# Softmax row statistics crossed between partition quadrants by VectorE instead of a TensorE product, and a new order of ScalarE's exponentials and roundings

## The chip, the core and the metric

The kernel runs on one core of a Trainium2 chip. The metric is the device time of one execution in microseconds (us). Three runs of the kernel before gave 2883.12, 2887.05 and 2887.52 us, median 2887.05 us.

Names in what follows: PE is TensorE's matmul row and PEld its weight load, DVE is VectorE, ACT is ScalarE, POOL is GpSimd, SP is the engine that issues most loads. Each engine runs its own instructions strictly in the order in which the program gives them, and engines wait for each other by semaphores. SBUF and PSUM have 128 partitions; a quadrant is 32 of them. L523 means line 523 of the kernel before.

## The reference, cut to what matters

A transformer block with adaptive layer norm. The change lies in the attention, where a softmax is taken over 512 keys:

```
h = layernorm(x) * (1 + ca) + sa
q = (h @ wq) as 32 heads of 128
k, v = the last 512 of 2048 cached positions, 16 heads, each used by 2 heads of q
p = softmax(q k^T * 128**-0.5)          # 2048 queries x 512 keys, per head
x = x + ga * ((p v) @ wo)
h = layernorm(x) * (1 + cb) + sb
x = x + gb * (relu(h @ W_gate) * (h @ W_up)) @ W_down
```

All data are float32. The kernel splits each operand of a product into a rounded part and a rest (hi and lo) and adds three products (hi hi, lo hi, hi lo), so each logical product is three matmuls.

## The kernel before, in words

The attention is cut into 128 units: a head and a block of 512 queries (32 heads, 4 blocks). The second half of the time is the gated MLP, which the change does not touch. All engines' orders are written out by hand; only the semaphores between them are put in by the framework. A list of timed steps (`step(name, t, ...)`, run by `run(u, k)` up to time 10u+k) puts the rest of the work (weight cuts, layer norms, gates of `wo`, MLP preparation) between the fixed parts of a unit.

One unit u, in the order of the loop at L1613:

- `s_half(u, 0)` and `(u, 1)` (L487): the scores, transposed, keys on partitions and queries on the free axis, in two PSUM tiles of 128 x 2 x 512 (pool psS, two buffers). Behind each, DVE takes a maximum with a 32x32 transposing reduction (L500), after which partition p of quadrant a holds, for column b, the maximum over the keys of that quadrant of query 32b + (p mod 32).
- `max_pre(u)` (L504): a small maximum over the four key tiles (L508), and the result spread into four masked copies, one per quadrant (L509).
- `sum_pre(u-1)` (L512): the same transposing reduction (L515) over the partial sums of the exponentials of the unit before.
- `qproj(u+1)`: 14 matmuls (L423) that make the next unit's queries.
- `spread(u)` (L519): one float32 product with the constant `quad` (L523), 80 columns. It adds up partitions that are equal modulo 32, so each quadrant receives what the four held: 64 columns for the masked maxima and 16 for the sums. It is PE's only work of this kind, and it stands in PE's order behind the 14 matmuls of `qproj`.
- `max_bc(u)` (L536): DVE's maximum over the four columns groups (L538), the reciprocal of the sums of u-1 (`sum_inv`, L528), and a 32x32 transpose that broadcasts the maximum to 128 x 512 (L551). For the units 0 to 3 and 127 (`by_pe`) the maximum is split into hi and lo (L544, L545), transposed (L546), rounded by ACT (L549) and subtracted by PE (L564).
- a piece of the output projection `wo` (12 matmuls, L637), `pv_half(u-1, 0)` (L610 to L612).
- `exp_half(u, 0)` and `(u, 1)` (L559): DVE subtracts the maximum (L568), ACT takes the exponential (L570). `hi_half` (L555) is ACT's rounding (L557); that of half 0 stands in ACT's order between the two exponentials, that of half 1 behind both.
- `sum_bc(u-1)` (L530): the broadcasting transpose of the reciprocal (L533); `q_lo(u+1)` (L477): the rest of the next queries (L479), which the next scores need; `ksum_op` (L579): DVE adds two of the four key tiles (L583), then POOL the other two (L586).
- `pv_half(u-1, 1)`, a second piece of `wo`, `o_mul(u-1)` (L618), then `lo_half` (L575): POOL subtracts the rounded from the exact exponentials (L577), 128 x 1024 per half. The product with v of unit u, in the unit after, needs them (L612).

PSUM pool psM has two buffers, taken in turn by `qps` (next queries), `qm` (the tile of the spread) and `pv`.

Of the kernel before, what the change touches and what calls it, by code (L numbers as in the profile page):

```python
# [28 lines left out]
PE0, PE1, MLP0 = 4, 1, 8  # L29
# [4 lines left out]
def kernel(  # L34
# [13 lines left out]
    nc = tc.nc  # L48
# [3 lines left out]
    cp = ctx.enter_context(tc.tile_pool(name="cp", bufs=1))  # L52
# [6 lines left out]
    bp = ctx.enter_context(tc.tile_pool(name="bp", bufs=3))  # L59
    op = ctx.enter_context(tc.tile_pool(name="op", bufs=3))  # L60
    xp = ctx.enter_context(tc.tile_pool(name="xp", bufs=3))
    sp = ctx.enter_context(tc.tile_pool(name="sp", bufs=2))
# [13 lines left out]

    ones = cp.tile([P, P], F32, name="ones")
    nc.vector.memset(ones, 1.0)

    ints = bp.tile([P, P], I32, tag="bc", name="ints")  # L80
    quad = cp.tile([P, P], F32, name="quad")
    nc.gpsimd.iota(ints, pattern=[[1, P]], base=P, channel_multiplier=-1)
    nc.vector.tensor_scalar(ints, ints, 31, None, op0=ALU.bitwise_and)
    nc.vector.tensor_scalar(quad, ints, 0.0, None, op0=ALU.is_equal)
    inta = bp.tile([P, 4], I32, tag="bc", name="inta")
    mask = cp.tile([P, 4], F32, name="mask")
    nc.gpsimd.iota(inta, pattern=[[-32, 4]], base=0, channel_multiplier=1)
    nc.vector.tensor_scalar(inta, inta, 5, None, op0=ALU.arith_shift_right)
    nc.vector.tensor_scalar(mask, inta, 0.0, None, op0=ALU.is_equal)

    intc = bp.tile([P, P], I32, tag="bc", name="intc")
    minus = cp.tile([P, P], F32R, name="minus")
# [355 lines left out]
    NU = HKV * NQB * 2  # L448
# [30 lines left out]
        nc.vector.scalar_tensor_tensor(qlo[u], qst.pop(u)[0], SCALE, qhi[u].bitcast(F32),  # L479
                                       op0=ALU.mult, op1=ALU.subtract)  # L480

    st_, t4, t5, pt, hi_, lo_, bc, rb, rinv, ks_, pvps, done, o, bps = ({} for _ in range(14))

    def by_pe(u):
        return u < PE0 or u >= NU - PE1

    def s_half(u, h):  # L487
        g, qb, hd = unit(u)
        k = ks[g]
        t = psS.tile([P, 2, 512], F32, tag="s", name=f"s{u}_{h}")  # L490
        st_[u, h] = t
        for j in range(2):
            kt = 2 * h + j
            ps = t[:, j, :]
            nc.tensor.matmul(ps, k[:, kt, :], qhi[u], start=True, stop=False)  # L495
            nc.tensor.matmul(ps, k[:, 4 + kt, :], qhi[u], start=False, stop=False)  # L496
            nc.tensor.matmul(ps, k[:, kt, :], qlo[u], start=False, stop=True)  # L497
        if h == 0:
            t4[u] = sp.tile([P, 4, 16], F32, tag="t4", name=f"t4_{u}", bufs=1)
        nc.vector.tensor_reduce(t4[u][:, 2 * h:2 * h + 2, :].rearrange("p k b -> p (k b)"),  # L500
                                t.rearrange("p k (b j) -> p (k b) j", j=32),
                                axis=AX.X, op=ALU.max, apply_transpose=True)

    def max_pre(u):  # L504
        t5[u] = sp.tile([P, 5, 16], F32, tag="t5", name=f"t5_{u}", bufs=1)
        bps[u] = psM.tile([P, 512], F32, tag="mm", name=f"qm{u}")
        t = bps[u][:, 128:144]
        nc.vector.tensor_reduce(t, t4.pop(u).rearrange("p k b -> p b k"), axis=AX.X, op=ALU.max)  # L508
        nc.vector.tensor_tensor(t5[u][:, 0:4, :], mask[:, :, None].to_broadcast([P, 4, 16]),  # L509
                                t[:, None, :].to_broadcast([P, 4, 16]), op=ALU.mult)  # L510

    def sum_pre(u):  # L512
        if u + 1 == NU:
            t5[NU] = sp.tile([P, 5, 16], F32, tag="t5", name=f"t5_{NU}", bufs=1)
        nc.vector.tensor_reduce(t5[u + 1][:, 4, :],  # L515
                                ks_.pop(u).rearrange("p (b j) -> p b j", j=32),
                                axis=AX.X, op=ALU.add, apply_transpose=True)

    def spread(u):  # L519
        a, b = (0 if u < NU else 4), (5 if u else 4)  # L520
        if u == NU:
            bps[u] = psM.tile([P, 512], F32, tag="mm", name=f"qm{u}")
        nc.tensor.matmul(bps[u][:, a * 16:b * 16], quad,  # L523
                         t5.pop(u)[:, a:b, :].rearrange("p a b -> p (a b)"), start=True, stop=True)

    def sum_inv(u):
        r = rinv[u] = sp.tile([P, 16], F32, tag="ri", name=f"ri{u}", bufs=1)
        nc.vector.reciprocal(r, bps[u + 1][:, 64:80])  # L528

    def sum_bc(u):  # L530
        r = rinv.pop(u)
        rb[u] = bp.tile([P, 512], F32, tag="bc", name=f"rb{u}")
        nc.vector.transpose(rb[u].rearrange("p (b j) -> p b j", j=32),  # L533
                            r[:, :, None].to_broadcast([P, 16, 32]))

    def max_bc(u):  # L536
        r = bps[u][:, 256:272] if by_pe(u) else sp.tile([P, 16], F32, tag="r", name=f"r{u}", bufs=1)
        nc.vector.tensor_reduce(r, bps[u][:, :64].rearrange("p (a b) -> p b a", a=4), axis=AX.X, op=ALU.max)  # L538
        if u:
            sum_inv(u - 1)  # L540
        m = bp.tile([P, 512], F32, tag="bc", name=f"mb{u}")
        if by_pe(u):
            rr = sp.tile([P, 16, 2], F32R, tag="rr", name=f"rr{u}", bufs=1)
            nc.vector.tensor_copy(rr[:, :, 0], r)  # L544
            nc.vector.tensor_sub(rr[:, :, 1], r, rr[:, :, 0].bitcast(F32))  # L545
            nc.vector.transpose(m.rearrange("p (b s t) -> p b s t", s=2, t=16),  # L546
                                rr.bitcast(F32)[:, :, :, None].to_broadcast([P, 16, 2, 16]))
            bc[u] = bp.tile([P, 512], F32R, tag="bc", name=f"mr{u}")
            nc.scalar.copy(bc[u], m)  # L549
        else:  # L550
            nc.vector.transpose(m.rearrange("p (b j) -> p b j", j=32),  # L551
                                r[:, :, None].to_broadcast([P, 16, 32]))
            bc[u] = m

    def hi_half(u, h):  # L555
        hi_[u, h] = pp.tile([P, 2, 512], F32R, tag="hi", name=f"hi{u}_{h}")
        nc.scalar.copy(hi_[u, h], pt[u, h])  # L557

    def exp_half(u, h):  # L559
        t = st_.pop((u, h))  # L560
        p = pp.tile([P, 2, 512], F32, tag="p", name=f"p{u}_{h}")
        if by_pe(u):
            for j in range(2):
                nc.tensor.matmul(t[:, j, :], minus, bc[u], start=False, stop=True,  # L564
                                 skip_group_check=True)
            nc.scalar.activation(p, t, AF.Exp, bias=0.0, scale=1.0)
        else:
            nc.vector.tensor_tensor(p, t, bc[u][:, None, :].to_broadcast([P, 2, 512]),  # L568
                                    op=ALU.subtract)
            nc.scalar.activation(p, p, AF.Exp, bias=0.0, scale=1.0)  # L570
        pt[u, h] = p
        if h == 0:
            hi_half(u, 0)

    def lo_half(u, h):  # L575
# [949 lines left out]
    mlp = mlp_slots()  # L1525

    def last_unit():
        spread(NU)
        sum_inv(NU - 1)
        sum_bc(NU - 1)  # L1530
        o_mul(NU - 1)

# [64 lines left out]
    def run(u, k):  # L1597
        t = 10 * u + k
        while sched and sched[-1][0] <= t:
            fn, args = sched.pop()[2:]  # L1600
            fn(*args)
# [11 lines left out]
    for u in range(NU):  # L1613
        run(u, 0)
        if u > 1 and u % 2 == 0:
            o_hi(u - 2)
            o_lo(u - 2)
        s_half(u, 0)
        s_half(u, 1)
        run(u, .5)  # L1620
        max_pre(u)
        if u:
            sum_pre(u - 1)
        run(u, 1)
        if u + 1 < NU:
            qproj(u + 1, 0, 14)
        else:
            piece(at[10 * u + 1])
            pv_part(u - 1, False)
        run(u, 2)  # L1630
        spread(u)
        max_bc(u)
        if u + 1 < NU:
            q_hi(u + 1)
        run(u, 3)
        if 10 * u + 3 in at:
            piece(at[10 * u + 3])
        if u > 1 and u % 2:
            o_hi(u - 2)
            o_lo(u - 2)  # L1640
        run(u, 4)
        if u + 1 == NU:
            pv_part(u - 1, True)
        elif u:
            pv_half(u - 1, 0)
        flush(pend_act)
        exp_half(u, 0)
        flush()
        run(u, 5)
        exp_half(u, 1)  # L1650
        if u:
            sum_bc(u - 1)
        if u + 1 < NU:
            q_lo(u + 1)
        ksum_op(u, 0)
        ksum_op(u, 1)
        run(u, 6)
        if 0 < u < NU - 1:
            pv_half(u - 1, 1)
        if 10 * u + 6 in at:  # L1660
# [67 lines left out]
```

## Time and profile before

The profiled execution took 2884.48 us; its span from the first to the last instruction is 2882.7 us, the rest of 1.8 us lies around it. The attention ends at about 1632 us.

| what | before |
|---|---|
| median of 3 runs | 2887.05 us |
| profiled execution, its span | 2884.48 us, 2882.7 us |
| granted TensorE clock, mean | 0.997 |
| ACT busy | 1496.2 us (52%) |
| L500 transposing maximum on DVE | 256 x 1244 ns |
| L568 subtraction of the maximum on DVE | 246 x 1218 ns |
| L570 exponential on ACT | 246 x 1056 ns |
| L557 rounding on ACT | 256 x 1051 ns |
| L577 subtraction for lo on POOL | 256 x 2399 ns |

A row of groups reads: line, engine, operation, output<-inputs, shapes, count, then busy us and mean ns of one, then the engine's idle time just before these instructions and what ended it. A row of the waits reads: engine, tile and line that waited, what it waited for, us in total, times, longest. A row of the timeline reads: start us, length us, engine, line, operation, output<-inputs, shapes, count of merged instructions, and in brackets the idle time before with what ended it.

### The profile page before, as it was taken

What the parts mean: (1) busy time and instruction counts of PE and PEld (TensorE: products, weight loads), DVE (VectorE), ACT (ScalarE), POOL (GpSimd) and SP (SyncE); (2) the same over time, 40 slices, a digit from 0 to 9 for tenths busy, and PEclk for the clock granted to TensorE, in tenths of its full rate; (3) what the DMA queues carried; (4) which work ended last, traced back from release to release, by engine and by line L of the source; (5) the groups of instructions that cost most, each with busy time, mean ns of one, the idle gap of its engine ahead of it and who ended that gap; (6) DMA issues with size and microseconds to landing.
All of it is one profiled execution on the core that took longest, in us unless ns stands there. A gap on an engine that the chain in (4) does not pass through costs nothing.

```text
span 2882.7 us, 41271 instructions
## 1 busy us (share of the span) xinstructions
PE 2839.4 (98%) x15214; PEld 2476.9 (86%) x15214; DVE 2149.1 (75%) x2967; ACT 1496.2 (52%) x2105; POOL 2115.0 (73%) x1564
## 2 busy tenths in 40 slices
PE   6999999999999999999999999999999999999999
PEld 5788888888888888888888888888888888888888
DVE  7778788888878888777889756676677466666666
ACT  5666666666676666666656444444444222222221
POOL 5688888888888889776778666787787356656553
PEclk9999999999999999999999999999999999999999
DMA  4012222222223223322244456666667944444442
GB/s 161 23 46 70 72 101 83 71 90 99 97 83 100 92 64 135 103 71 87 66 131 145 149 216 218 233 243 232 228 228 256 354 160 156 154 154 155 160 153 106
DMA packets 164362, 399.59 MB, mean 139 GB/s; under 512 B 15040, under 2 KB 61888, under 8 KB 164160
## 3 DMA queue, kind: packets, MB, share of 16 engines
q1 hardware_dynamic: 132912, 284.84, 30.1%
q10 hardware_dynamic: 31248, 112.11, 9.9%
q8 instruction: 121, 1.98, 0.3%
q14 instruction: 81, 0.66, 0.1%
HBM read 271.16 MB, written 154.57 MB: 148 GB/s over the span
## 4 chain that ended last, share of the span: by engine, by line
PE 90%; POOL 3%; DVE 2%; ACT 2%; DMA 2%; issue 1%; SPq 0%; ACTq 0%; POOLq 0%; DVEq 0%
PE gu L981 26%; PE wo L637 13%; PE qps L423 13%; PE md L637 8%; PE st_P L1083 6%; PE s L497 4%; PE s L496 4%; PE s L495 4%; PE pv L612 4%; PE pv L611 4%; PE pv L610 4%; PE qm L523 1%; POOL lo L577 1%; ACT p L570 0%; DVE ws L788 0%
## 5 line engine op out<-in xcount | busy, mean ns | idle before, releaser
L577 POOL TENSOR_TENSOR lo<-p,hi 128x1024 fp32r<-128x1024 f32 x256 | 608.7, 2399 | 1.1 <-ACT hi L557 1.1
L586 POOL TENSOR_TENSOR ks<-ks,p 128x512 f32<-128x512 f32 x256 | 343.8, 1343 | 270.6 <-ACT p L570 212.6
L500 DVE TRANSPOSE_TENSOR_REDUCE t<-s 128x32 f32<-128x1024 f32 x256 | 316.6, 1244 | 136.9 <-PE s L497 125.6
L981 PE MATMUL gu<-hop_B,wop 128*128 128x512 f32 x1512 | 374.5, 391 | 0.2 <-DMA wop<-wk_P 0.2
L981 PEld LDWEIGHTS gu<-hop_B,wop 128*128 128x128 f32 x1512 | 275.0, 188 | 50.5 <-ACT lflh L966 0.9
L981 PE MATMUL gu<-hop_T,wop 128*128 128x512 f32 x1260 | 316.0, 391 | 0.0
L423 PE MATMUL qps<-hTa,wA 128*128 128x512 f32 x1288 | 311.4, 392 | 4.2 <-DVE hTa L371 2.1
L637 PE MATMUL wo<-woga,ohi 128*128 128x288 f32 x1472 | 306.5, 301 | 0.0
L568 DVE TENSOR_TENSOR p<-s,mb 128x1024 f32<-128x1024 f32 x246 | 290.2, 1218 | 4.1
L423 PEld LDWEIGHTS qps<-hTa,wA 128*128 128x128 f32 x1288 | 242.8, 189 | 57.4 <-DVE hTa L371 4.2
L557 ACT CAST hi<-p 128x1024 fp32r<-128x1024 f32 x256 | 269.1, 1051 | 7.1
L570 ACT ACTIVATE p<-p 128x1024 f32<-128x1024 f32 x246 | 259.8, 1056 | 7.6 <-DVE p L568 7.3
L637 PE MATMUL md<-wogb,hhi 128*128 128x288 f32 x1280 | 258.9, 295 | 3.6 <-DVE acc L648 2.6
L981 PEld LDWEIGHTS gu<-hop_T,wop 128*128 128x128 f32 x1260 | 227.8, 188 | 38.9
L475 ACT ACTIVATE qhi<-qps 128x512 fp32r<-128x512 f32 x128 | 76.5, 597 | 340.4 <-PE qps L423 340.4
L637 PEld LDWEIGHTS wo<-woga,ohi 128*128 128x128 f32 x1472 | 239.2, 189 | 7.3
L648 DVE TENSOR_TENSOR acc<-md,acc 128x576 f32<-128x576 f32 x160 | 120.7, 755 | 160.8 <-PE md L637 160.3
L637 PEld LDWEIGHTS md<-wogb,hhi 128*128 128x128 f32 x1280 | 212.2, 188 | 16.6 <-DVE acc L648 4.3
L637 PE MATMUL wo<-woga,olo 128*128 128x288 f32 x736 | 217.4, 295 | 0.3 <-POOL olo L626 0.2
L1092 DVE TENSOR_TENSOR acc<-st_P,acc 128x576 f32<-128x576 f32 x160 | 121.0, 757 | 128.0 <-PE st_P L1083 128.0
L637 PE MATMUL md<-wogb,hlo 128*128 128x288 f32 x640 | 188.6, 295 | 0.0
L646 ACT COPY acc<-wo 128x576 f32<-128x576 f32 x233 | 148.2, 636 | 66.8 <-PE wo L637 60.4
(274 smaller groups left out, 7107.2 us busy)
## 6 DMA issues: line engine op xcount, KB each, us to landing
wop<-wk_P SPq DMA_DIRECT2D x133, 640.0 KB
wk_P<-wop ACTq DMA_DIRECT2D x119, 640.0 KB
wr<-wlay SPq DMA_DIRECT2D x68, 384.0 KB
rogb<-wd SPq DMA_DIRECT2D x68, 288.0 KB
againq<-akq SPq DMA_DIRECT2D x18, 640.0 KB
rwA<-wq SPq DMA_DIRECT2D x32, 320.0 KB
wlay<-wg SPq DMA_DIRECT2D x36, 256.0 KB
roga<-wo SPq DMA_DIRECT2D x32, 288.0 KB
```

What stands on the lines that cost most here:

```text
L423: return [lambda i=i, a=a, b=b: nc.tensor.matmul(ps, a, b, start=(i == 0), stop=(i == n - 1)) for i, (a, b) in enumerate(ops)]
L500: nc.vector.tensor_reduce(t4[u][:, 2 * h:2 * h + 2, :].rearrange("p k b -> p (k b)"), t.rearrange("p k (b j) -> p (k b) j", j=32), axis=AX ...
L557: nc.scalar.copy(hi_[u, h], pt[u, h])
L568: nc.vector.tensor_tensor(p, t, bc[u][:, None, :].to_broadcast([P, 2, 512]), op=ALU.subtract)
L570: nc.scalar.activation(p, p, AF.Exp, bias=0.0, scale=1.0)
L577: nc.gpsimd.tensor_sub(lo_[u, h], pt[u, h], hi_[u, h].bitcast(F32))
L586: nc.gpsimd.tensor_tensor(ks_[u], ks_[u], p[:, j, :], op=ALU.add)
L637: nc.tensor.matmul(ps[:, half, :H2], a[:, sl], w[b][:, cs], start=(n == 0 and seed is None), stop=(n == 5), skip_group_check=seed is not None)
L646: nc.scalar.copy(av, ps[:, :, :H2])
L981: nc.tensor.matmul(ps, a, c, start=s not in heir(m) and i == 0 and s not in seeds_of(m), stop=i == len(ops) - 1, skip_group_check=True)
L1083: nc.tensor.matmul(ps[:, j, :H2], x[:, sl], w[:, y, :], start=n == 0 and not second, stop=n == 2, skip_group_check=True)
L1092: nc.vector.tensor_tensor(t, ps[:, :, :H2], t, op=ALU.add)
```

## The change

It has three parts.

1. The constants `quad` and `mask` go, with two iotas of POOL and four small operations of DVE at the start. `max_pre`, `spread` and `sum_inv` go: per unit L508, L509, the product L523 and L538. In their place `cross(u)` does the crossing on DVE with reductions: the four per-tile maxima (16 columns each) and the sums (16 columns) of quadrants 2 and 3 are moved beside those of 0 and 1 (one operation, 64 partitions, 80 elements), then those of quadrant 1 beside quadrant 0 (32 partitions, 160 elements); quadrant 0 takes the maximum of 256 elements to 16 and the sum of 64 to 16; the two results (32 elements) are moved to quadrant 1, and then from 0 and 1 to 2 and 3. A move is a maximum over an axis of length one. `t4` and `t5` become one SBUF tile of 128 x 21 x 16.
2. `cross(u)` and `max_bc(u)` stand in the program right behind `sum_pre(u-1)`, ahead of `qproj(u+1)` and of the timed steps of 10u+1 and 10u+2. The reciprocal moves into `sum_bc`, behind both subtractions L568, in place, and directly ahead of the transpose L533.
3. For the units 5 to 125, ACT's rounding of half 0 moves behind the exponential of half 1.

```diff
+        nc.vector.tensor_reduce(t5[u][:, 8 * h:8 * h + 8:4, :],
                                 t.rearrange("p k (b j) -> p (k b) j", j=32),
                                 axis=AX.X, op=ALU.max, apply_transpose=True)
...
-    def max_pre(u):
...
-    def spread(u):
...
-    def sum_inv(u):
...
+    def move(dst, src):
+        nc.vector.tensor_reduce(dst, src[..., None], axis=AX.X, op=ALU.max)
+
+    def cross(u):
+        t = t5.pop(u)
+        v = t[:, 0:20, :].rearrange("p (k a) b -> p k a b", a=4)[:, (0 if u < NU else 4):(5 if u else 4)]
+        move(v[0:64, :, 1, :], v[64:128, :, 0, :])
+        move(v[0:32, :, 2:4, :], v[32:64, :, 0:2, :])
+        r = rr_[u] = t[:, 15:21:5, :]
+        if u < NU:
+            nc.vector.tensor_reduce(r[0:32, 1, :], t[0:32, 0:16, :].rearrange("p n b -> p b n"), axis=AX.X, op=ALU.max)
+        if u:
+            nc.vector.tensor_reduce(r[0:32, 0, :], t[0:32, 16:20, :].rearrange("p n b -> p b n"), axis=AX.X, op=ALU.add)
+        w = slice(0 if u else 1, 2 if u < NU else 1)
+        move(r[32:64, w, :], r[0:32, w, :])
+        move(r[64:128, w, :], r[0:64, w, :])
 
     def sum_bc(u):
-        r = rinv.pop(u)
+        r = rr_.pop(u + 1)[:, 0, :]
+        nc.vector.reciprocal(r, r)
...
     def max_bc(u):
-        r = bps[u][:, 256:272] if by_pe(u) else sp.tile([P, 16], F32, tag="r", name=f"r{u}", bufs=1)
-        nc.vector.tensor_reduce(r, bps[u][:, :64].rearrange("p (a b) -> p b a", a=4), axis=AX.X, op=ALU.max)
-        if u:
-            sum_inv(u - 1)
+        r = rr_[u][:, 1, :]
...
+    def late_hi(u):
+        return PE0 < u < NU - 2
...
-        if h == 0:
+        if h == 0 and not late_hi(u):
             hi_half(u, 0)
...
-        max_pre(u)
         if u:
             sum_pre(u - 1)
+        cross(u)
+        max_bc(u)
         run(u, 1)
...
-        spread(u)
-        max_bc(u)
         if u + 1 < NU:
             q_hi(u + 1)
...
         exp_half(u, 1)
+        if late_hi(u):
+            hi_half(u, 0)
```

More of the change, by code (lines that the diff above doesn't have):

```diff
@@ L78 @@
     nc.vector.memset(ones, 1.0)
[L80 to L89, printed above, removed]
     intc = bp.tile([P, P], I32, tag="bc", name="intc")
@@ L480, in q_lo @@
                                        op0=ALU.mult, op1=ALU.subtract)
-    st_, t4, t5, pt, hi_, lo_, bc, rb, rinv, ks_, pvps, done, o, bps = ({} for _ in range(14))
+    st_, t5, pt, hi_, lo_, bc, rb, rr_, ks_, pvps, done, o = ({} for _ in range(12))
     def by_pe(u):
@@ L498, in s_half @@
         if h == 0:
-            t4[u] = sp.tile([P, 4, 16], F32, tag="t4", name=f"t4_{u}", bufs=1)
-        nc.vector.tensor_reduce(t4[u][:, 2 * h:2 * h + 2, :].rearrange("p k b -> p (k b)"),
+            t5[u] = sp.tile([P, 21, 16], F32, tag="t5", name=f"t5_{u}", bufs=1)
+        nc.vector.tensor_reduce(t5[u][:, 8 * h:8 * h + 8:4, :],
                                 t.rearrange("p k (b j) -> p (k b) j", j=32),
                                 axis=AX.X, op=ALU.max, apply_transpose=True)
-    def max_pre(u):
[L505 to L510, printed above, removed]
@@ L512, in sum_pre @@
     def sum_pre(u):
         if u + 1 == NU:
-            t5[NU] = sp.tile([P, 5, 16], F32, tag="t5", name=f"t5_{NU}", bufs=1)
-        nc.vector.tensor_reduce(t5[u + 1][:, 4, :],
+            t5[NU] = sp.tile([P, 21, 16], F32, tag="t5", name=f"t5_{NU}", bufs=1)
+        nc.vector.tensor_reduce(t5[u + 1][:, 16, :],
                                 ks_.pop(u).rearrange("p (b j) -> p b j", j=32),
                                 axis=AX.X, op=ALU.add, apply_transpose=True)
-    def spread(u):
[L520 to L524, printed above, removed]
@@ L526, in sum_inv @@
-    def sum_inv(u):
-        r = rinv[u] = sp.tile([P, 16], F32, tag="ri", name=f"ri{u}", bufs=1)
-        nc.vector.reciprocal(r, bps[u + 1][:, 64:80])
+    def move(dst, src):
[13 more added lines that the diff above has]
+        move(r[64:128, w, :], r[0:64, w, :])
@@ L1527, in last_unit @@
     def last_unit():
-        spread(NU)
-        sum_inv(NU - 1)
+        cross(NU)
         sum_bc(NU - 1)
```

## The prediction, made before the changed kernel had run

> **What bounds the kernel now.** First the page's busy shares and the chain that ended last:
>
> ```profile
> span 2882.7 us, 41271 instructions
> PE 2839.4 (98%) x15214; PEld 2476.9 (86%) x15214; DVE 2149.1 (75%) x2967; ACT 1496.2 (52%) x2105; POOL 2115.0 (73%) x1564
> ...
> PE 90%; POOL 3%; DVE 2%; ACT 2%; DMA 2%; issue 1%; SPq 0%; ACTq 0%; POOLq 0%; DVEq 0%
> ```
>
> Then the waits, those of PE first, then the long ones of DVE and POOL that belong to the attention:
>
> ```profile
> PE mps L170 <- DVE wmb L1306: 15.2, 1, 15.2
> PE qm L523 <- DVE t L515: 3.2, 4, 1.5
> ...
> PE pv L612 <- POOL lo L577: 1.3, 2, 0.7
> ```
>
> ```profile
> POOL ks L586 <- ACT p L570: 212.6, 101, 6.6
> ...
> DVE t L500 <- PE s L497: 125.6, 101, 2.6
> ...
> DVE r L538 <- PE qm L523: 108.9, 123, 1.4
> ```
>
> PE is the bound: after the start (15.2 us) it waits a few us in all, and the chain lies on it. So PE work that goes is time that goes, as long as no other engine makes PE wait instead. DVE's spare time in the attention is what it waits for PE: 125.6 + 108.9 = 234 us over 128 units, 1.8 us a unit. The change spends some of it. So I read one ordinary unit, DVE alone, from one L500 to the next:
>
> ```profile
> 603.27 2.61 DVE L500 TRANSPOSE_TENSOR_REDUCE t<-s 128x32 f32<-128x1024 f32 x2 [1.17 <-PE s L497]
> 605.91 0.28 DVE L508 TENSOR_REDUCE qm<-t 128x16 f32<-128x64 f32 x1
> ...
> 606.37 0.70 DVE L515 TRANSPOSE_TENSOR_REDUCE t<-ks 128x16 f32<-128x512 f32 x1
> 607.99 0.22 DVE L538 TENSOR_REDUCE r<-qm 128x16 f32<-128x64 f32 x1 [0.93 <-PE qm L523]
> ...
> 608.30 0.67 DVE L551 STREAM_TRANSPOSE mb<-r 128x512 f32<-128x512 f32 x1
> 609.00 2.36 DVE L568 TENSOR_TENSOR p<-s,mb 128x1024 f32<-128x1024 f32 x2
> 611.27 0.70 DVE L533 STREAM_TRANSPOSE rb<-ri 128x512 f32<-128x512 f32 x1
> 611.89 0.65 DVE L479 SCALAR_TENSOR_TENSOR qlo<-qps,qhi 128x512 fp32r<-128x512 f32 x1
> 612.47 0.67 DVE L583 TENSOR_TENSOR ks<-p 128x512 f32<-128x512 f32 x1
> 613.06 0.68 DVE L618 TENSOR_TENSOR rb<-pv,rb 128x512 f32<-128x512 f32 x1
> 615.35 1.25 DVE L500 TRANSPOSE_TENSOR_REDUCE t<-s 128x32 f32<-128x1024 f32 x1 [1.61 <-PE s L497]
> ```
>
> The unit takes 615.35 - 603.27 = 12.08 us. DVE is idle 0.93 us before L538 and 1.61 us at the end. The maximum's broadcast L551 waits for the product, and the product for PE's 14 matmuls ahead of it.
>
> **The product that goes.** PE's own order around it, and a passage from 512-column matmuls into `wo` without it:
>
> ```profile
> 606.92 0.85 PE L423 MATMUL qps<-hTa,wA 128*128 128x512 f32 x3
> 607.61 0.35 PE L523 MATMUL qm<-t,quad 128*128 128x80 f32 x2
> ...
> 608.11 0.29 PE L637 MATMUL wo<-woga,olo 128*128 128x288 f32 x1
> ```
>
> ```profile
> 611.96 0.39 PE L612 MATMUL pv<-lo,kv 128*128 128x512 f32 x1
> ...
> 612.44 0.29 PE L637 MATMUL wo<-woga,olo 128*128 128x288 f32 x1
> ```
>
> Three matmuls end at 607.77 and the last is 0.39 long, so it starts at 607.38. From there to the first `olo` matmul 0.73 us pass with the product, 0.48 without. It costs 0.25 us. L523 has 258 instructions, two to a product, 129 products: **-32 us**. PE's waits at L523 for the sums, 3.2, go as such: **-3 us**. An ordinary unit would then take 11.83 us.
>
> **What DVE gets.** No row shows a reduction over an axis of length one, nor one that shifts quadrants. The same reduction has two lengths here, L500 with 1024 elements and L515 with 512:
>
> ```profile
> L500 DVE TRANSPOSE_TENSOR_REDUCE t<-s 128x32 f32<-128x1024 f32 x256 | 316.6, 1244 | 136.9 <-PE s L497 125.6
> ...
> L515 DVE TRANSPOSE_TENSOR_REDUCE t<-ks 128x16 f32<-128x512 f32 x128 | 90.1, 704 | 0.0
> ...
> L508 DVE TENSOR_REDUCE qm<-t 128x16 f32<-128x64 f32 x128 | 35.3, 276 | 4.4
> ...
> L284 DVE BATCH_NORM_STATS2 stb<-acc 128x6 f32<-128x288 f32 x16 | 6.4, 444 | 0.4 <-ACT acc L646 0.4
> ...
> L161 DVE COPY macc<-macc 128x64 f32<-128x64 f32 x2 | 0.4, 178 | 0.0
> ```
>
> 540 ns for 512 elements is 1.055 ns each, with 164 ns fixed; L538 (64 elements, 0.22 us) fits. The six operations of `cross` have 80, 160, 256, 64, 32 and 32 elements: 0.25 + 0.33 + 0.43 + 0.23 + 0.20 + 0.20 = 1.64 us. In the unit above a dependent operation starts 0.03 us after the one before (L568 behind L551; I take 0.04), an independent one 0.09 before its end (L533 behind L568). L515 now follows L500 directly: 605.79 to 606.49. Five dependent gaps and one overlap bring the end of `cross` to 606.49 + 1.64 + 0.20 - 0.09 = 608.24, and L551 to 608.28: **where it was** (608.30). DVE's wait for the product pays for the three added operations.
>
> The reciprocal, 0.25 us, now stands between L568 and L533, which must wait for it: all from L533 on is 0.3 us later. L500 to the end of L618 was 10.47 us and becomes 10.77; against 11.83 that leaves 1.06 us spare (1.61 before). Bounds on 10.77: if each of the six costs 0.05 us less than its line, as the copy L161 does (64 elements, 0.178 us), 10.45. If each has L508's excess (276 against 232 ns) and the strided maximum of 256 elements pays that excess per element, 0.5 more, 11.27; if reductions that write every element take twice per element, another 0.3, 11.6. I take 10.77, by L538, whose sizes are the nearest.
>
> **When PE notices.** The first thing that PE needs from DVE is `qlo` for the next scores: L479 ends at 612.54, and the scores use it here:
>
> ```profile
> 614.22 0.40 PE L497 MATMUL s<-qlo,kv 128*128 128x512 f32 x1
> ```
>
> 1.68 us of margin; minus 0.25 and 0.3 it is 1.13. DVE may be late by that much without cost. Lateness grows in a unit by its extra DVE work minus 1.06, never below nothing; what exceeds 1.13 at `qlo`, PE waits. Extra work is not even. A gate L222 is 0.749 us in the median, the longest 2.366:
>
> ```profile
> L222 DVE TENSOR_TENSOR roga<-roga,mrow x32: 742/749/2366, 69.3 to 1161.1; 128x576 f32<-128x576 f32 x32
> ```
>
> One of these alone, or a modulation step of like size, fits. One that meets POOL, or two in neighbouring units, do not:
>
> ```profile
> 576.23 1.53 DVE L583 TENSOR_TENSOR ks<-p 128x512 f32<-128x512 f32 x1
> ...
> 578.29 1.54 DVE L222 TENSOR_TENSOR roga<-roga,mrow 128x576 f32<-128x576 f32 x1
> ```
>
> L583 is 0.86 longer there than in the ordinary unit, L222 comes on top, 2.3 us of extra: 1.2 us late, with the next gate a unit away. There are 16 pairs of gates, one for each pair of heads; if some 12 of them cost about 0.8 us, that is 10 us. The layer norm statistics of four units (L284, 16 of 444 ns, and their aggregation, some 2 us of extra in a unit) are 2 us by the same sum. Last, the eight units from 1509 us on, where each holds one or two combinations of h (L851) and DVE has hardly any spare now:
>
> ```profile
> 1557.35 2.37 DVE L500 TRANSPOSE_TENSOR_REDUCE t<-s 128x32 f32<-128x1024 f32 x2
> ...
> 1561.48 0.22 DVE L538 TENSOR_REDUCE r<-qm 128x16 f32<-128x64 f32 x1 [0.57 <-PE qm L523]
> 1561.62 0.25 DVE L528 RECIPROCAL ri<-qm 128x16 f32<-128x16 f32 x1
> 1561.79 0.66 DVE L551 STREAM_TRANSPOSE mb<-r 128x512 f32<-128x512 f32 x1
> ```
>
> L500's end to L551 takes 2.07 us there against 2.40 after the change, plus 0.3 for the reciprocal: about 0.6 late a unit, and PE 0.25 early. Eight units by 0.85, less 1.13 of margin: 6 us. Together **+18 us** of new waits of PE (at 10.45 the same sum gives 9, at 11.27 some 40, at 11.6 some 70).
>
> **ScalarE's order.** POOL's sums wait for the second exponential (212.6 us in 101 units, above):
>
> ```profile
> 610.95 1.06 ACT L570 ACTIVATE p<-p 128x1024 f32<-128x1024 f32 x1
> ...
> 613.00 1.05 ACT L570 ACTIVATE p<-p 128x1024 f32<-128x1024 f32 x1
> ```
>
> It would end at 613.05 in place of 614.05. But L586 also needs L583, which ends 0.3 later at 613.43, so POOL gains 0.6 us, not 1.0, and then waits for DVE. The rounding of half 0 ends where the exponential ended, long before `lo` reads it; behind it on ACT stand the `wo` evacuations, whose total ahead is the same. PE waits 1.3 us for `lo` now, so little is to be won directly. It covers PE's 0.25 us and DVE's 0.3, which would otherwise make `lo` late. I cost it at nothing. The removed setup lies ahead of PE's 15.2 us wait at the start and is worth a few tenths at most; `qm` leaving psM's rotation gives `pv` more room, and PE's waits there are part of the few us; I cost both at nothing.
>
> One danger is in it: POOL's earlier sums (two L586 a unit) run when L222 and the modulation steps are issued, and the two rows of 1.5 us above show what such a meeting costs. If all quiet ones meet (0.8 us each), the waits are 26, not 18. The Trainium skill, "SBUF — State Buffer", section "Who interferes with whom", has the rule: a VectorE instruction with two SBUF inputs and a GpSimd one exclude each other for a whole instruction, in order of issue. By that rule the sum would be 8 us worse; the rows bear it out where both engines are busy, and a reduction, with one input, is free of it.
>
> **Sum** against the profiled execution of 2884.48 us (span 2882.7): -32 - 3 + 18 = -17, 2867.5 us. The median of the runs shown is 2.6 us above that execution, so **2870 us**.
>
> **Rivals.** (1) DVE stays hidden everywhere: -35, so 2852 us. For it: 1.06 us spare in ordinary units; against it: the last eight units, with no idle time but the 0.57. Likely if the operations cost the low end. (2) **DVE becomes the pace, slower than before.** Place: `cross` and the reciprocal in every unit. Each 0.1 us by which the six operations together exceed 1.64 us comes off the spare 1.06; at 11.3 (0.5 us over) the new waits are as large as the 35 us won, and at 11.4 to 11.6 they are 50 to 70: 2902 to 2922, 2909 as its middle. For it: the only small reduction out of SBUF, L508, is above the line. The Trainium skill, "VectorE: DVE Perf Modes", section "Rules for kernel authors", speaks for it: in chained operations it asks for the fewest, and calls the reduction the slowest kind. Here six take the place of three; no run here shows it yet. (3) The meetings with POOL, 8 us: 2878. (4) The exponentials' order gives POOL nothing, because L583 is what it waits for, and `lo` comes late in units with weight cuts on POOL, some 30 by 0.25: 2878.
>
> **How the numbers follow.** Forecast 0.45 (2860 to 2880), rival 1 0.18, rival 2 0.24 with a tail down to 2885, rival 3 0.08, rival 4 0.05. Range 2850 to 2898: it leaves out most of rival 2 and little else. A difference of 0.2% (5.8 us) is about what a measurement here can tell from none: slower than 2893, 0.19; between 2881 and 2893, 0.08 (the low tail of rival 2, the high ones of 3 and 4); faster, 0.73.
>
> **What would show it.** Right: `wo` follows `qps` directly on PE; L551 starts about 5 us after its unit's first L500; six operations of 0.2 to 0.43 us; units of 11.83 us; POOL's sums released by L583; PE waits at L497 for `qlo`, most from 1509 us on. Wrong: operations of `cross` over 2.1 us in all, ordinary units at 12 us with no idle time on DVE, or PE waiting for `lo`.

## The result, and the profile after

The changed kernel takes 2893.53 us in the median of 9 runs (2891.84 to 2900.61), the kernel before, run beside it, 2886.35 (9 runs, 2879.69 to 2887.71). Over all these runs the ratio is 1.0034, 95% interval 1.0025 to 1.0043. Forecast was 2870. The change costs 7 us by the medians, 10 by that ratio, where it was to gain 17.

The page of the changed kernel, busy shares and the chain:

```profile
span 2898.0 us, 41016 instructions
PE 2825.2 (97%) x14956; PEld 2447.2 (84%) x14956; DVE 2307.9 (80%) x3351; ACT 1478.0 (51%) x2105; POOL 2123.3 (73%) x1562
...
PE 58%; DVE 8%; POOL 5%; issue 2%; DMA 2%; ACT 1%; ACTq 0%; SPq 0%; POOLq 0%; DVEq 0%
```

PE has 258 instructions fewer. Its share of the chain fell from 90% to 58%, while DVE's rose from 2% to 8% and POOL's from 3% to 5%; the shares listed add up to 76%, and the page does not say who holds the rest. The waits of the same execution, those of PE, then POOL's and DVE's in the attention:

```profile
PE s L552 <- ACT mr L534: 12.4, 5, 3.7
PE s L486 <- DVE qlo L468: 8.0, 11, 1.6
PE wo L625 <- DVE lfb L329: 5.0, 4, 1.3
...
PE pv L600 <- POOL lo L565: 5.0, 8, 0.7
```

```profile
POOL ks L574 <- ACT hi L542: 138.9, 74, 4.6
POOL ks L574 <- DVE ks L571: 101.1, 46, 5.8
...
DVE t L489 <- PE s L486: 58.5, 69, 2.2
```

DVE's idle time at the scores went from 125.6 to 58.5 us and its 108.9 at the product are gone: the slack was used up, in some units wholly. PE's wait for `lo`, 1.3 us before, is now 5.0. POOL's additions (L574) were to be released by L571. The list names ScalarE's rounding in 74 of the waits, but an addition does not read what the rounding writes, and in these 74 as in the 46 put down to L571 it starts 0.13 to 0.15 us behind L571's end. An ordinary unit, DVE (below) and PE's passage into `wo`:

```profile
601.99 2.62 DVE L489 TRANSPOSE_TENSOR_REDUCE t<-s 128x32 f32<-128x1024 f32 x2
604.53 0.67 DVE L496 TRANSPOSE_TENSOR_REDUCE t<-ks 128x16 f32<-128x512 f32 x1
605.24 0.57 DVE L501 TENSOR_REDUCE t<-t 64x80 f32<-64x80 f32 x2
605.84 0.58 DVE L510 TENSOR_REDUCE t<-t 32x16 f32<-32x256 f32 x1
606.46 0.25 DVE L512 TENSOR_REDUCE t<-t 32x16 f32<-32x64 f32 x1
606.75 0.39 DVE L501 TENSOR_REDUCE t<-t 32x32 f32<-32x32 f32 x2
607.17 0.71 DVE L536 STREAM_TRANSPOSE mb<-t 128x512 f32<-128x512 f32 x1
```

```profile
603.84 2.65 PE L412 MATMUL qps<-hTa,wA 128*128 128x512 f32 x11
606.33 0.42 PE L625 MATMUL wo<-woga,ohi 128*128 128x288 f32 x2
```

`wo` follows `qps` at once, the broadcast of the maximum (L536, before L551) starts 5.18 us into the unit (5.03 before), and the ordinary units take 11.83 us to the hundredth (of the units 60 to 104, 23 between 11.83 and 11.85). There the prediction came true. The loss lies elsewhere. The table holds the lengths of stretches, each from the start of a unit's first L489 (before: L500) to another's; "end" is from unit 127 to the first matmul of the gated MLP (`gu`), "MLP" from there to the end of the span. Forecast is what the prediction's terms give for the stretch.

| kernel | to unit 0 | 0-6 | 6-105 | 105-119 | 119-127 | end | MLP |
|---|---|---|---|---|---|---|---|
| before | 39.4 | 88.6 | 1204.3 | 176.3 | 97.3 | 9.5 | 1267.3 |
| after | 39.9 | 90.4 | 1191.8 | 181.7 | 108.3 | 10.9 | 1275.0 |
| difference | +0.4 | +1.8 | -12.5 | +5.4 | +11.1 | +1.4 | +7.7 |
| forecast | 0 | -4.7 | -14.8 | -1.5 | +4 | -0.2 | 0 |

The attention is 7.6 us longer, close to the difference of the medians (7.2). The MLP's 7.7 us are not the change's: this execution is 6.2 us above its own median, and the twelve profiled executions of this study took 1267.0 to 1275.0 us for that stretch, whose code is the same in all. Much of what makes them differ is seen in the changed kernel's execution; DVE, then PE:

```profile
1939.95 6.07 DVE L776 TENSOR_TENSOR wr<-wr,wr 128x768 f32<-128x768 f32 x1
...
1947.21 0.94 DVE L776 TENSOR_TENSOR ws<-wr,wr 128x768 f32<-128x768 f32 x1
```

```profile
1940.19 0.43 PE L625 MATMUL md<-wogb,hhi 128*128 128x288 f32 x2
...
1946.75 0.55 PE L625 MATMUL md<-wogb,hhi 128*128 128x288 f32 x2 [2.40 <-DVE acc L636]
...
1948.05 0.68 PE L625 MATMUL md<-wogb,hhi 128*128 128x288 f32 x2
```

One subtraction of weights takes 6.07 us in place of 0.94 while POOL works without a gap, the accumulation behind it (L636) is late, PE stands for 2.40 us, and a pair of matmuls then takes 0.68 in place of 0.43 for some microseconds (granted clock 0.91 in the 20 us around). Executions with no pause of PE over 1 us in the MLP took 1267.0 to 1268.0 us for it, those with one 1267.3 to 1272.8, those with two 1272.7 to 1275.0 (one of e9's two is a wait for a DMA). Not every pause has slow matmuls behind it: before's one pause had none (granted clock 1.00), and its MLP took 1267.3. So what follows is read from the attention's stretches.

### The profile page after: what moved, and what is told of

Read it like the earlier page. It is cut to its first block, busy times and chain, and to the rows that moved or that the text cites. A ratio compares the mean times of both kernels' runs of the same rounds, so it can differ in the third digit from the quotient of the medians.

```text
span 2898.0 us, 41016 instructions
## 1 busy us (share of the span) xinstructions
PE 2825.2 (97%) x14956; PEld 2447.2 (84%) x14956; DVE 2307.9 (80%) x3351; ACT 1478.0 (51%) x2105; POOL 2123.3 (73%) x1562
## 4 chain that ended last, share of the span: by engine, by line
PE 58%; DVE 8%; POOL 5%; issue 2%; DMA 2%; ACT 1%; ACTq 0%; SPq 0%; POOLq 0%; DVEq 0%
PE gu L969 24%; PE md L625 7%; PE st_P L1071 6%; PE wo L625 6%; PE qps L412 5%; PE s L486 2%; PE s L485 2%; PE s L484 2%; PE pv L600 1%; PE pv L599 1%; PE pv L598 1%; DVE t L489 1%; POOL lo L565 1%; DVE p L556 1%; POOL wop L748 1%
## 5 line engine op out<-in xcount | busy, mean ns | idle before, releaser
L574 POOL TENSOR_TENSOR ks<-ks,p 128x512 f32<-128x512 f32 x256 | 350.4, 1369 | 262.6 <-ACT hi L542 138.9
L489 DVE TRANSPOSE_TENSOR_REDUCE t<-s 128x32 f32<-128x1024 f32 x256 | 313.1, 1237 | 67.6 <-PE s L486 58.5
L558 ACT ACTIVATE p<-p 128x1024 f32<-128x1024 f32 x246 | 251.5, 1054 | 42.0 <-DVE p L556 40.2
L625 PEld LDWEIGHTS wo<-woga,ohi 128*128 128x128 f32 x1472 | 248.0, 189 | 18.2 <-POOL woga L171 3.5
L542 ACT CAST hi<-p 128x1024 fp32r<-128x1024 f32 x256 | 257.6, 1040 | 0.4
L636 DVE TENSOR_TENSOR acc<-md,acc 128x576 f32<-128x576 f32 x160 | 120.7, 755 | 171.0 <-PE md L625 170.7
L614 POOL TENSOR_TENSOR olo<-rb,ohi 128x512 fp32r<-128x512 f32 x128 | 165.9, 1296 | 13.7 <-ACT ohi L610 13.7
```

Of the source, the lines that this page charges most:

```text
L489: nc.vector.tensor_reduce(t5[u][:, 8 * h:8 * h + 8:4, :], t.rearrange("p k (b j) -> p (k b) j", j=32), axis=AX.X, op=ALU.max, apply_transp ...
L574: nc.gpsimd.tensor_tensor(ks_[u], ks_[u], p[:, j, :], op=ALU.add)
L614: nc.gpsimd.tensor_sub(olo[u], o.pop(u), ohi[u].bitcast(F32))
L625: nc.tensor.matmul(ps[:, half, :H2], a[:, sl], w[b][:, cs], start=(n == 0 and seed is None), stop=(n == 5), skip_group_check=seed is not None)
```

## The experiments

Stretches of all of them, as above, each from one profiled execution:

| kernel | to unit 0 | 0-6 | 6-105 | 105-119 | 119-127 | end | MLP | median us | ratio to before, interval |
|---|---|---|---|---|---|---|---|---|---|
| e1, ACT's order back | 39.3 | 90.6 | 1194.7 | 181.9 | 108.4 | 10.8 | 1267.3 | 2896.80 | 1.0035 [1.0022, 1.0048] |
| e2, ACT's order alone | 40.0 | 84.8 | 1202.3 | 175.8 | 101.4 | 9.5 | 1270.1 | 2889.15 | 1.0009 [0.9999, 1.0019] |
| e3, crossing at the old place | 41.5 | 89.6 | 1191.7 | 175.6 | 108.4 | 10.9 | 1271.5 | 2887.93 | 1.0010 [1.0001, 1.0020] |
| e4, no crossing | 39.6 | 85.9 | 1174.9 | 171.4 | 95.3 | 10.3 | 1267.0 | 2846.69 | 0.9865 [0.9850, 0.9880] |
| e5, maximum in PSUM | 39.5 | 89.0 | 1192.6 | 181.7 | 108.4 | 11.0 | 1272.8 | 2896.39 | 1.0036 [1.0022, 1.0051] |
| e6, additions left out | 40.1 | 90.6 | 1192.2 | 181.7 | 124.4 | 10.9 | 1271.0 | 2913.02 | one run |
| e7, mixed | 39.8 | 90.0 | 1192.7 | 179.3 | 97.2 | 9.5 | 1272.9 | 2884.18 | 0.9997 [0.9987, 1.0008] |
| e8, h early | 41.1 | 90.6 | 1191.6 | 181.7 | 98.5 | 12.8 | 1268.0 | 2888.23 | 1.0010 [1.0000, 1.0020] |
| e9, both | 39.8 | 89.4 | 1191.7 | 175.6 | 98.5 | 13.4 | 1272.7 | 2882.68 | 0.9989 [0.9980, 0.9998] |
| e10, mixed, constant later | 41.0 | 89.4 | 1192.6 | 176.7 | 97.2 | 9.5 | 1269.2 | 2881.57 | 0.9983 [0.9974, 0.9992] |

The kernel before, run beside them, had medians of 2885.39 (e1 to e4), 2886.25 (e5 to e7), 2884.88 (e8, e9) and 2886.89 us (e10).

**e1 and e2: is it ScalarE's order?** The changed kernel with the old order, and the kernel before with the new one.

```diff
     def late_hi(u):
-        return PE0 < u < NU - 2
+        return False
```

```diff
# e2, against the kernel before
-        if h == 0:
+        if h == 0 and not late_hi(u):
             hi_half(u, 0)
...
         exp_half(u, 1)
+        if late_hi(u):
+            hi_half(u, 0)
```

> The changed kernel with ScalarE's old order (the rounding of half 0 between the two exponentials). Theory A (VectorE is the pace in the units that carry extra work: start, layer norm units, last eight; the meetings with GpSimd are a part): the last eight units fall from 13.7 to about 13.0 us each because the first combination of h no longer meets the sums on GpSimd, some 5 us, and lo comes later elsewhere, 2 to 4 us back: 2888 to 2893. Rival B (the new order of ScalarE is the loss, since it starts the sums right behind L571 and so beside VectorE's two-input operations): without it the crossing brings most of what was forecast, 2876 or less.

> The kernel before with nothing but ScalarE's new order. Theory A: VectorE has 1.6 us spare in an ordinary unit and 0.6 in the last eight; the meetings with GpSimd cost a few us at most, 2885 to 2890. Rival B: the new order alone costs most of the 7 to 16 us by which the changed kernel misses its forecast, 2893 or more.

Measured 2896.8 and 2889.15 us. The order is not the loss: with the old one the changed kernel keeps its 108.4 us in the last eight units and loses 2.9 us in the middle (1194.7 beside 1191.8). My expectation that those units would fall to 13.0 us was wrong. Alone, the new order gains 2.0 us in the middle and costs 4.1 us in the last eight units, and its median can't be told from before's. The 4.1 us are the first sight of what e4, e6 and e8 take apart: DVE (of e2) in one of these units.

```profile
1576.26 1.47 DVE L854 TENSOR_TENSOR lfb<-lfb,lfb 128x512 f32<-128x512 f32 x1
1577.65 1.78 DVE L854 TENSOR_TENSOR h<-h,h 128x512 f32<-128x512 f32 x1
```

L854 is the line of `h0_comb`, the combination of h, in that kernel; it takes 0.67 us where nothing runs beside it (e8).

**e3: is it the place of the crossing?** `cross` and `max_bc` behind the timed steps, where `spread` and `max_bc` had stood.

```diff
         if u:
             sum_pre(u - 1)
-        cross(u)
-        max_bc(u)
         run(u, 1)
...
         run(u, 2)
+        cross(u)
+        max_bc(u)
```

> The changed kernel with cross and max_bc put back to where spread and max_bc stood, behind the next queries' matmuls and the timed steps of 10u+1 and 10u+2. Theory A: in units 113, 114, 116 and 117 TensorE waits 1.25 us each for the affine L329 of a layer norm, which now stands behind the crossing on VectorE; put ahead of it again these units fall from 14.25 to 13.0 us, 5 us in all, the rest stays: about 2888. Rival C (the place does not matter, only the amount of VectorE's work): 2893.

Measured 2887.93: as expected. The units 113 to 119 fall from 82.4 to 76.3 us, the others stay. DVE in the changed kernel (first), and in e3 at the same work:

```profile
1438.10 0.67 DVE L496 TRANSPOSE_TENSOR_REDUCE t<-ks 128x16 f32<-128x512 f32 x1
...
1440.77 0.71 DVE L536 STREAM_TRANSPOSE mb<-t 128x512 f32<-128x512 f32 x1
1441.40 0.77 DVE L329 TENSOR_SCALAR lfb<-ltb,mcol,mcol 128x512 f32<-128x512 f32 x1
```

```profile
1437.42 0.67 DVE L496 TRANSPOSE_TENSOR_REDUCE t<-ks 128x16 f32<-128x512 f32 x1
1438.01 0.77 DVE L329 TENSOR_SCALAR lfb<-ltb,mcol,mcol 128x512 f32<-128x512 f32 x1
```

PE's wait in the changed kernel that ends with it:

```profile
1442.23 0.54 PE L625 MATMUL wo<-againo,ohi 128*128 128x288 f32 x2 [1.27 <-DVE lfb L329]
```

L329 reads the PSUM tile that `wo` needs next. It was a timed step of 10u+1; the crossing and the broadcast, 2.7 us, now stand ahead of it, and PE waits 1.3 us in each of four units. These are the 5.0 us of the list of waits.

**e4: what is the product worth, and what does DVE's crossing take back?** No crossing at all: each quadrant uses its own maximum and sum (so the softmax is another one), and four of the six operations are left out.

```diff
-        move(v[0:64, :, 1, :], v[64:128, :, 0, :])
-        move(v[0:32, :, 2:4, :], v[32:64, :, 0:2, :])
...
-            nc.vector.tensor_reduce(r[0:32, 1, :], t[0:32, 0:16, :].rearrange("p n b -> p b n"), axis=AX.X, op=ALU.max)
+            nc.vector.tensor_reduce(r[:, 1, :], t[:, 0:16:4, :].rearrange("p n b -> p b n"), axis=AX.X, op=ALU.max)
...
-        move(r[32:64, w, :], r[0:32, w, :])
-        move(r[64:128, w, :], r[0:64, w, :])
```

> The changed kernel with the crossing left out: every quadrant keeps its own maximum and sum, so the softmax is not over all keys. It has neither the product on TensorE nor the four moves on VectorE. Theory A: the product was worth 0.25 us a unit and its waits, and nothing but VectorE's added work took it back: 2850, ordinary units 11.83 us, the last eight about 11.9. Rival D (something else in the change costs time, in the MLP after the attention too): 2865 or more, with the MLP's part longer than before.

Measured 2846.69, 38.7 us below before. So the product with its waits (and ScalarE's new order) is worth some 38 us, a little more than the 35 of the prediction, and the crossing takes back 45.6 of the attention: 17 in the units 6 to 105, 10 in 105 to 119, 13 in 119 to 127, 4.5 in 0 to 6.

**e5: the first units.** In the units 0 to 3 and 127 the maximum is split into two parts. It had lain in PSUM; the change put it into SBUF. e5 puts it back.

```diff
+        if by_pe(u) and u < NU:
+            rm = rps[u] = psM.tile([P, 512], F32, tag="mm", name=f"rm{u}")
+            nc.vector.tensor_reduce(rm[0:32, 0:16], t[0:32, 0:16, :].rearrange("p n b -> p b n"), axis=AX.X, op=ALU.max)
+            move(rm[32:64, 0:16], rm[0:32, 0:16])
+            move(rm[64:128, 0:16], rm[0:64, 0:16])
...
-        r = rr_[u][:, 1, :]
+        r = rps[u][:, 0:16] if by_pe(u) else rr_[u][:, 1, :]
```

> After, but in the units 0 to 3 and 127 the crossed maximum is written to a PSUM tile (taken in turn from psM, where the product's tile was), so that the cast and the subtraction that split it (L529, L530) read PSUM again. Theory A, that these two wait in SBUF for POOL: they take 0.1 to 0.2 us each in every such unit, units 0 to 6 take 87.5 to 88.2 us in place of 90.39 (units 1 and 2 give back 1.6 and 1.3), unit 127 up to the first gu 9.5 in place of 10.9, and the time falls by 3 to 4 us from 2893, to 2889 to 2891. Theory B, that the longer chain of the crossing makes mr late there: units 0 to 6 stay above 89.8 and the time at 2893.

The two operations became short again; DVE, then POOL at that time, of the changed kernel, and DVE of e5:

```profile
56.16 1.07 DVE L529 CAST rr<-t 128x16 fp32r<-128x16 f32 x1
...
70.90 1.19 DVE L530 TENSOR_TENSOR rr<-t,rr 128x16 fp32r<-128x16 f32 x1
```

```profile
52.48 4.72 POOL L565 TENSOR_TENSOR lo<-p,hi 128x1024 fp32r<-128x1024 f32 x2
...
70.78 1.28 POOL L614 TENSOR_TENSOR olo<-rb,ohi 128x512 fp32r<-128x512 f32 x1
```

```profile
56.34 0.18 DVE L536 CAST rr<-rm 128x16 fp32r<-128x16 f32 x1
56.55 0.17 DVE L537 TENSOR_TENSOR rr<-rm,rr 128x16 fp32r<-128x16 f32 x1
```

Sixteen elements took over 1 us: L529 ends at 57.23, POOL's `lo` at 57.20; L530 at 72.09, POOL's `olo` at 72.06. But the gain is 1.4 us in the units 0 to 6, where 2.2 to 2.9 were expected; unit 127 did not move, and the time (2896.39) did not fall. PE now waits 5.4 us at `pv` for that tile to come free (psM has two buffers). The two operations are shorter for certain, the gain of time is not: e7 and e10, which have the same step, take 90.0 and 89.4 us there, and unit 3, which is the same in before and e2, took 16.32 and 14.50 us.

**e6: the last eight units, POOL's additions left out.** In the units 119 to 126 the sums hold half of the keys.

```diff
-        else:
+        elif not 119 <= u < 127:
             for j in range(2):
                 nc.gpsimd.tensor_tensor(ks_[u], ks_[u], p[:, j, :], op=ALU.add)
```

> After, but in the units 119 to 126 POOL's two additions of the sums are left out (the sums hold half of the keys there). Theory A, that a unit there is long because h0_comb (L839) and its second part (L861) meet POOL's additions: both are back at about 0.67 us, the units 122 to 125 fall from 13.73 to 12.3 to 12.6 us and the stretch 119 to 127 from 108.3 to 97 to 100. Theory B, that DVE's longer chain (the crossing and the reciprocal) alone does it: the units stay at 13.5 or more.

Both theories missed: the units became longer, 13.73 to about 15.9 us. The traces show why. DVE and POOL of the changed kernel at the end of a unit, then the same of e6:

```profile
1581.51 1.47 DVE L839 TENSOR_TENSOR lfb<-lfb,lfb 128x512 f32<-128x512 f32 x1
1582.90 1.77 DVE L839 TENSOR_TENSOR h<-h,h 128x512 f32<-128x512 f32 x1
```

```profile
1581.13 2.99 POOL L574 TENSOR_TENSOR ks<-ks,p 128x512 f32<-128x512 f32 x2 [3.09 <-DVE ks L571]
1584.08 5.23 POOL L565 TENSOR_TENSOR lo<-p,hi 128x1024 fp32r<-128x1024 f32 x2
```

```profile
1576.47 2.40 DVE L861 TENSOR_TENSOR hy_T<-h,hy_T 32x512 fp32r<-32x512 f32 x1
1578.90 2.77 DVE L839 TENSOR_TENSOR lfb<-lfb,lfb 128x512 f32<-128x512 f32 x1
```

```profile
1575.92 2.41 POOL L565 TENSOR_TENSOR lo<-p,hi 128x1024 fp32r<-128x1024 f32 x1 [4.89 <-ACT hi L542]
```

With the additions away POOL took up `lo`, whose instructions are twice as long, and DVE's two operations grew with them, from 1.35 and 1.67 us to 2.40 and 2.77. Their ends show how. L861 ends at 1578.87, 0.54 us behind POOL's `lo` (1578.33); in the changed kernel the second L839 ends at 1584.67, 0.55 us behind POOL's additions (1584.12). So each waits for the end of POOL's instruction and then takes some 0.55 us of its own. That L861's 2.40 stands beside POOL's 2.41 is chance: it was issued 0.55 us behind `lo`.

**e8: the same without the meeting.** DVE's steps of that stretch (h0_comb, and h0_cut's small subtraction) stand ahead of the first partial sum. POOL's additions wait for that sum, so POOL is idle while they run.

```diff
+        run(u, 5.5)
         ksum_op(u, 0)
         ksum_op(u, 1)
...
-            step("h0.a", H + at_, h0_comb, *H0_COMB[key], t)
+            step("h0.a", H + at_ - 2.5, h0_comb, *H0_COMB[key], t)
...
-            step("h0.c", H + at_ + (6 if t == 2 else 4 if at_ // 10 % 2 else 6),
+            step("h0.c", H + at_ + (3.5 if t == 2 else 4 if at_ // 10 % 2 else 6),
```

> After, but in the units 119 to 126 (and where the same steps stand before them) DVE's two parts of the MLP preparation, h0_comb (L839) and the small subtraction of h0_cut (L861), stand ahead of the first partial sum (L571) in place of behind the output's product (L606). POOL's additions wait for L571, so POOL is idle when the two run. The left-out additions of the run before showed that DVE's instruction lasts as long as POOL's beside it (2.40 beside 2.41, in place of 1.35 beside 1.29). Theory A, that these meetings make the units long: L839 and L861 take 0.67 us each, the units 122 to 125 take 12.1 to 12.6 us in place of 13.73, the stretch 119 to 127 97 to 101 in place of 108.3, and the time falls by 7 to 11 us, to 2883 to 2887. Theory B, that DVE's longer chain alone does it: the units stay above 13.2 and the time at 2891 or more.

DVE, then POOL, of e8:

```profile
1576.17 0.67 DVE L839 TENSOR_TENSOR lfb<-lfb,lfb 128x512 f32<-128x512 f32 x1
1576.77 0.68 DVE L839 TENSOR_TENSOR h<-h,h 128x512 f32<-128x512 f32 x1
1577.37 0.69 DVE L571 TENSOR_TENSOR ks<-p 128x512 f32<-128x512 f32 x1
```

```profile
1578.19 2.67 POOL L574 TENSOR_TENSOR ks<-ks,p 128x512 f32<-128x512 f32 x2 [2.03 <-DVE ks L571]
```

The units 122 to 125 take 12.3 to 12.5 us, about 0.3 over before, and the eight together 98.5, 9.9 less. The time, 2888.23, is 1.2 us above the range expected: the end is 1.9 us longer.

The meetings alone are not the loss, though. e4 has them too; its DVE in one of these units:

```profile
1552.94 1.37 DVE L855 TENSOR_TENSOR hy_T<-h,hy_T 32x512 fp32r<-32x512 f32 x1
1554.33 1.70 DVE L833 TENSOR_TENSOR lfb<-lfb,lfb 128x512 f32<-128x512 f32 x1
```

These are L861 and L839 of the changed kernel, as long as there (1.36 and 1.69 in the unit at 1595 us). But e4 has no crossing, and its eight units take 95.3 us. It takes both: the crossing and the meetings together are more than DVE has time for. In the changed kernel it is never idle for more than 0.04 us between 1509 and 1609 us, and PE waits for it; with either taken away the loss is nearly gone.

**e7, e9 and e10: can the gain be kept?** e9 is e3 and e8 together. e7 and e10 let DVE cross up to unit 107, with the maximum in PSUM in the units 0 to 3, and from 108 on use the product of PE and the old order of ScalarE. For want of SBUF the constant of the product lies where `ones` lay, and is made when that is done: in e7 ahead of the crossing of unit 106, in e10 behind the output's product of 106 and 107.

```diff
# e7 and e10, the core
+    def product(u):
+        return u >= 108
...
+        if product(u):
+            max_pre(u)
         if u:
             sum_pre(u - 1)
+        if not product(u):
+            cross(u)
+            max_bc(u)
...
+        if product(u):
+            spread(u)
+            max_bc(u)
```

> DVE crosses the quadrants in the units up to 107 as in the changed kernel (with the maximum in PSUM in units 0 to 3, and ScalarE's new order), and from unit 108 on, with the layer norms, the combinations of h and the end, the product of PE is back with the old order; its constant is made in unit 106. If the loss lies where DVE has no time to spare and the gain in the ordinary units, the units 6 to 108 keep their gain of 12.5 us, 108 on takes what it took before (61.6, 77.5, 97.3 us and 9.5), units 0 to 6 about 88, and the median is 2870 to 2877, below both kernels. The rival, that the lateness carries over or that the gain of the middle hangs on something else: 2882 or more.

> The run before together with the crossing at its old place, behind the 14 matmuls and the timed steps (as in the third experiment). If the two losses are separate, they add up: the units 113 to 119 take 76.3, 119 to 127 97 to 101, and the median is 2893 - 6 - 9 = 2878 (2875 to 2882), below both kernels. If they are one lateness seen twice, it stays at 2884 or more.

> As the mixed kernel of the seventh run (VectorE crosses up to unit 107, the product of PE from 108 on), but the constant of the product is made behind the output's product of units 106 (GpSimd) and 107 (VectorE) in place of ahead of the crossing of unit 106, where it cost 3.25 us. Then unit 106 takes 11.83 us again, the attention is about 10 us shorter than before, and the median is 2878 to 2882 beside 2885 to 2886 of before. If the constant costs as much there, or if the rest of the gain was given back in the second half, it stays at 2884.

e7 missed its expectation of 2870 to 2877 (2884.18). The stretches from 108 on are those of before, as expected, but unit 106 took 15.08 us in place of 11.83 for the constant, and the first units kept their loss. e9 takes 2882.68, just above its range, and the two gains do add up by stretch (175.6 and 98.5). e10 takes 2881.57, within its range, and is the best that I found: 5.3 us below before, its interval clear of it. In these three the attention of the profiled execution is 7 to 9 us shorter than before, the median only 2 to 5; whether such kernels meet more of the pauses in the MLP was not settled.

## Why the prediction was wrong, by its own steps

The prediction had -35 us for the product and its waits and +18 of new waits. In the attention, e4 puts the first at -38.0 and the second at +45.6. So what failed is the term of new waits: the place of the crossing and the first units, put at nothing, the last eight units, put at half, and the middle, put at 10 for 16.9.

- **The product, 0.25 us each: right.** Ordinary units of 11.83 us, and e4, which is rival 1 made real, takes 38.7 us off where 35 were forecast. The waits for `qlo` lie where they were forecast (4.5 of the 8.0 us after 1509 us). One of its signs of being wrong came too: PE waits for `lo`, 5.0 us, of which 2.9 after 1509 us.
- **The six operations, 1.64 us: 0.1 low.** The groups of the changed kernel:

```profile
L510 DVE TENSOR_REDUCE t<-t 32x16 f32<-32x256 f32 x128 | 75.2, 587 | 4.4
...
L501 DVE TENSOR_REDUCE t<-t 32x160 f32<-32x160 f32 x127 | 39.0, 307 | 4.4
L512 DVE TENSOR_REDUCE t<-t 32x16 f32<-32x64 f32 x128 | 32.5, 254 | 4.4
...
L501 DVE TENSOR_REDUCE t<-t 64x80 f32<-64x80 f32 x127 | 29.4, 231 | 4.4
L501 DVE TENSOR_REDUCE t<-t 64x32 f32<-64x32 f32 x127 | 22.8, 180 | 4.4
L501 DVE TENSOR_REDUCE t<-t 32x32 f32<-32x32 f32 x128 | 22.5, 176 | 4.4
```

Together 1.735 us. The moves came out 0.02 below the line, the maximum of 256 elements 0.15 above it. L489 to the end of L606 is 10.95 us (forecast 10.77), which leaves 0.88 spare: far from 11.3, where rival 2 put its point. Rival 2, DVE as the pace in every unit, is refuted; the kernel became slower all the same, in other places. (The middle of rival 2's 2902 to 2922 is 2912, not 2909; nothing hangs on it.)

- **Gates, +10 in the middle: the net right, both sizes low.** The units 6 to 105 gained 12.5 us where the terms give 14.8. By e4 the product and its waits, with ScalarE's order, were worth 29.4 there (forecast 24.8) and the new waits 16.9 (forecast 10). Which gates make them was not taken apart.
- **The place of the crossing, not priced: 6 us.** The prediction wrote that L551 stays "where it was" and priced ordinary units only. In the units 113 to 117 the edit moved the broadcast past timed steps of 10u+1, one of which frees a tile of PE. The row stood in the trace of before (L340 at 1434.83, L538 at 1436.72). e3 shows it. With the 2 us of the layer norm statistics the stretch 105 to 119 came out at +5.4 against -1.5.
- **The last eight units, +6 new waits: 13** (11.1 us longer than before, 13.0 longer than e4). This is the failed step of largest size. The prediction counted DVE's longer chain (0.85 a unit) and no new meeting with POOL. Before, in most of these units one of the two operations ran before POOL's additions and one met them:

```profile
1591.53 0.68 DVE L873 TENSOR_TENSOR hy_T<-h,hy_T 32x512 fp32r<-32x512 f32 x1
1592.23 1.69 DVE L851 TENSOR_TENSOR lfb<-lfb,lfb 128x512 f32<-128x512 f32 x1
```

Now both meet them: POOL's additions are released by L571, as forecast, and the two operations come soon behind it. On top of the crossing that is more than DVE's spare time: without the meetings (e8) 9.9 us come back, without the crossing (e4) all 13. Rival 3 had the mechanism and its price (0.8 us), but tied it to the gates and the modulation steps and to ScalarE's order; e1 shows that the order is not needed for it.
- **The first units, no new waits priced: +1.8 us in place of -4.7.** The waits for L523 that were to go (3 us) were replaced by others: PE waits 12.4 us at L552 for the split maximum, 2.1 before. e4 puts the crossing at 4.5 us there, e5 the two short operations at 1.4 at most. The rest, and the 1.4 us at the end, which e5 does not touch and e10 does, go with the crossing; their cause stays open.
- **ScalarE's order, nothing: nearly right.** In the changed kernel it gains 2.9 us in the middle and costs nothing in the last eight units (e1). Alone it gains 2.0 and gives 4.1 back there (e2).

The Trainium skill, "SBUF — State Buffer", section "Who interferes with whom", says that the shared port is locked for a whole instruction, that a copy or cast can take it too, and that a reduction never contends. This case agrees on each: L861 of e6 ends 0.54 us behind the `lo` that it met, the cast 0.03 us behind POOL's, and L510 takes between 571 and 607 ns in all its 128 instances, while POOL runs beside 124 of them. The prediction cited the rule and then applied it to the gates and the modulation steps alone.

## What to carry to other kernels

When work moves onto an engine, read not the ordinary stage but each stage in which that engine has other work, and ask for every instruction behind the moved one what the other engines run at its new time and who waits for it. An instruction moved ahead of others is priced by those others. One that can be locked out costs the rest of its neighbour's time on top of its own, which hurts only where its engine has no time to spare (the changed kernel beside e4). A gain of 38 us on the bound engine was undone here, some 23 us of it in the last 22 units; using the new form only where slack exists (e10), or setting the order anew around it (e9), kept a part.

## What the runs showed that I had not expected

- Reductions over an axis of length one move data between quadrants at 176 ns for 32 elements and 307 for 160, and none of either shape varied by more than 5 ns. The strided maximum of 256 elements took 587 ns where the prediction's line gives 434.
- The broadcasting transpose of a maximum takes 712 ns out of the strided tile (L536) and took 665 out of a tile of its own (L551).
- A cast of 16 elements from SBUF to SBUF took 0.18 us in its median and 1.07 when POOL's instruction had to end first; from PSUM it took 0.18.
- After a pause of PE of 2.4 us, in some executions and not in others, a pair of matmuls took 0.68 us in place of 0.43 for some microseconds.
